# A long-convolution layer and an MLP on one Trainium2 core: wider PSUM pieces in front, an inverse transform with the data as weights, and the second layer norm moved into the MLP

## The chip, the cores and the metric

The kernel runs on one core of one Trainium2 chip. A core has five engines, each of which takes its own instructions strictly in program order: TensorE (PE in the profile, its weight loads PEld), VectorE (DVE), ScalarE (ACT), GpSimd (POOL) and SyncE (SP, which here only issues transfers). They meet through semaphores. Matrix products land in PSUM[...]; TensorE writes to it, VectorE and ScalarE read it[...]. All other tiles lie in SBUF. The metric is the time on the device in microseconds.

## The reference

Sequence S = 2048, width D = 512, MLP width 1376, all inputs bf16.

```python
x = A_q
k_shift = sum over t < 4 of k_pad[:, t:t+S, :] * shift_k[:, 3 - t]
kv = k_shift * v
y = irfft(rfft(kv, 2S) * rfft(ssm_k, 2S))[:S] + kv * ssm_D
h = x + layernorm(x) * y
out = h + relu(layernorm(h) @ w1) @ w2
```

So there is a causal long convolution of every channel with its own filter of 2048 taps, a gate by a layer norm of x, and an MLP behind a second layer norm. The layer norms have no weights of their own.

## The kernel before, in words

The convolution is a Fourier transform of length 4096 in two steps, written as matrix products. Each channel's 2048 times are seen as 32 rows of 64, and the transform goes over the rows (`stage1`), then over the 64 columns with the twiddle factors in the matrices `cc`, `cs` and `cn` (`stage2`). Two channels share the 128 partitions.

1. **Front.** `to_rows` (L195) turns the filter around with 64 transposes on TensorE. `stage1` (L207) transforms it, with four row groups of TensorE side by side: 64 matmuls per group `gb`, into four PSUM tiles of one bank, each copied to SBUF by ScalarE ("A") or VectorE ("D") as a string says. Between the groups, `taps` (L255) makes the four-tap convolution of k on TensorE, and VectorE multiplies it by v. `to_rows` and `stage1` then treat the product kv in the same way (with twice the columns, `wide`). `stage2` of the filter stands in between (L283 to L289): its results go to `kf` in pairs.
2. **Product** (L308 to L340). For each of 16 pairs of frequencies TensorE makes `u`, ScalarE copies a part of it for GpSimd (L317), VectorE and GpSimd multiply it by `kf` (L321), TensorE adds the parts up (L331), and ScalarE writes the result back to `kf` (L333).
3. **Inverse 1** (L389 to L400). 128 matmuls with `kf` as the weights and the two matrices `dre` and `dim` as the moving side; 32 copies to `bp`. Beside it the tables for the last step (`ecore`) are made: whole numbers by GpSimd and VectorE (`ec_turns`), sines by ScalarE (`ec_sins`). The loads of x, w1 and w2 are issued ahead of it on SP's queue.
4. **Inverse 2** (`inv2`, L412). For each of four quarters `q` of the tokens, 256 fp32 matmuls of 32x32 with the table as the weights; ScalarE copies the result, tokens in the partitions, to `zt`.
5. **Gate and MLP.** `ln1` makes the layer norm of x (statistics and normalising on VectorE, `rstd` on GpSimd), `gate` the residual, `hln_` the second layer norm, `transposes` (L466) turn it around on TensorE. `mlp1` and `mlp2` then run quarter by quarter, 44 matmuls of 512 columns each, and every output is added to its residual by VectorE (L501) and stored by SP. The transposes of the next quarter stand in the middle of `mlp2` as a `hook`.

The schedule is manual: on each engine the instructions run in the order in which the program writes them. So an instruction that waits holds everything that its engine has behind it. Dependencies between engines follow from the tiles that the instructions read and write, and a pool's number of buffers says how far a producer may run ahead. The framework puts in the waits.

Of the kernel before, what the change touches and what calls it, by code (L numbers as in the profile page):

```python
# [56 lines left out]
def kernel(  # L57
# [33 lines left out]
    psum = pl.push("psF", bufs=8, space=PSUM)  # L91
# [6 lines left out]
    dtab = consts.tile([P, DC, 64], BF16, name="dtab")  # L98
    for dp in range(2):
        src = bass.AP(tensor=A_ssm_D.tensor, offset=A_ssm_D.offset + 64 * dp, ap=[[0, 64], [P, DC], [1, 64]])  # L100
        nc.scalar.dma_start(out=dtab[64 * dp:64 * dp + 64, :, :], in_=src)
# [93 lines left out]
    def to_rows(src, q, fl, eng):  # L195
        pst = psum.tile([P, 8, P], BF16, tag="ps", name="pst")
        for i in range(8):
            nc.tensor.transpose(out=pst[:, i, :], in_=src[:, :, :, 8 * q + i], identity=ident[:])  # L198
        copy(eng, fl[:, :, :, 8 * q:8 * q + 8], pst[:].rearrange("p i (d g) -> p g d i", d=2))
# [7 lines left out]
    def stage1(fl, a_out, engs, between=None, wide=False):  # L207

        for gb in range(8):
            pss = [psum.tile([P, 8, 64], F32, tag="ps", name=f"ps1_{r}") for r in range(4)]  # L210
            for gi in range(8):
                for f, first in ((f1hi, True), (f1lo, False)):
                    for rg in range(4):
                        rows = slice(32 * rg, 32 * rg + 32)
                        w = 2 if wide and gi < 7 else 1
                        nc.tensor.matmul(out=pss[rg][:, gi:gi + w, :].rearrange("p g c -> p (g c)"),  # L216
                                         lhsT=fl[rows, 8 * gb + gi, :, :].rearrange("p d n -> p (d n)"),
                                         rhs=f[rows, 0:64 * w], start=first, stop=not first,
                                         tile_position=(32 * rg, 0), skip_group_check=wide)
            for rg in range(4):  # L220
                j0 = 64 * rg + 8 * gb
                copy(engs[(4 * gb + rg) % len(engs)], a_out[:, :, j0:j0 + 8], pss[rg][:].rearrange("p g c -> p c g"))
            if between is not None:
                between(gb)
# [23 lines left out]
    dre = consts.tile([P, 2, P], F32R, name="dre")  # L248
    dim = consts.tile([P, 2, P], F32R, name="dim")
# [5 lines left out]
    def taps(u):  # L255
        c, rg = divmod(u, DC)
        ps = psum.tile([P, CH], F32, tag="ps", name="pkv")
        for j in range(KS):
            nc.tensor.matmul(out=ps[:], lhsT=wdiag[:, rg, j, :], rhs=kT[c][:, rg, 16 - j:CH + 16 - j],  # L259
                             start=(j == 0), stop=(j == KS - 1))  # L260
        vv = vT[:, rg, CH * c:CH * c + CH]
        nc.vector.tensor_tensor(out=vv, in0=ps[:], in1=vv, op=ALU.mult)

    def two_taps(gb):
        taps(2 * gb)
        taps(2 * gb + 1)

    stage1(kfl, a1k, "ADAADADA", two_taps)
    for pq in halves:
        for dst, rho, blk, sgn in ((dre, 0, 0, 1.0), (dre, 1, 1, 1.0), (dim, 0, 1, -1.0), (dim, 1, 0, 1.0)):  # L270
            nc.gpsimd.tensor_single_scalar(out=dst[pq, rho, pq], in_=dsc[pq, blk, :], scalar=sgn / 2048, op=ALU.mult)
# [10 lines left out]
    dcol = dtab[:].rearrange("p r g -> p (r g)").unsqueeze(2).to_broadcast([P, 256, 2])  # L282
    for kp in range(16):  # L283
        ks = slice(2 * kp, 2 * kp + 2)
        ps = [psum.tile([P, 2, 256], F32, tag="ps", name=f"ps2k{s}") for s in range(2)]
        for s in range(2):
            stage2(ps[s], a1k, kp, s)
        nc.vector.tensor_tensor(out=kf[:, 0, :, ks], in0=ps[0][:].rearrange("p k j -> p j k"), in1=dcol, op=ALU.add)
        nc.scalar.copy(out=kf[:, 1, :, ks], in_=ps[1][:].rearrange("p k j -> p j k"))  # L289

    a1x = slotA.tile([P, 64, 256], F32R, tag="A", name="a1x")
    stage1(xfl, a1x, "ADADADAA", wide=True)
# [54 lines left out]
    xh = late.tile([P, NT, D], BF16, name="xh")  # L347
    for a, src in enumerate(_tokens(x_d, 0, NT)):
        nc.sync.dma_start(out=xh[32 * a:32 * a + 32, :, :].rearrange("p t d -> p (t d)"), in_=src)
    w1 = late.tile([P, DC, DFF], BF16, name="w1")  # L350
    w2 = late.tile([P, NFC, D], BF16, name="w2")
    nc.sync.dma_start(out=w1[:], in_=B_w1.rearrange("(c p) f -> p c f", p=P))
    nfull = DFF // P
    nc.sync.dma_start(out=w2[:, 0:nfull, :], in_=B_w2[0:nfull * P, :].rearrange("(c p) d -> p c d", p=P))
    if DFF % P:
        nc.sync.dma_start(out=w2[0:DFF % P, nfull, :], in_=B_w2[nfull * P:DFF, :])
    ecore = late.tile([P, 2, 64, 32], F32, name="ecore")
# [4 lines left out]
    rstd2 = late.tile([P, NT, 1], F32, name="rstd2")  # L362
    mhalf = late.tile([P, 4], F32, name="mhalf")
    nc.gpsimd.memset(mhalf[:], -0.5)
    tmpc = pl.push("tmpc", side="right")
    psum = pl.push("psI", bufs=8, space=PSUM)
    k1i = tmpc.tile([P, 1], I32, name="k1i")
    for s in range(0, P, 32):
        nc.gpsimd.iota(k1i[s:s + 32, :], pattern=[[0, 1]], base=1, channel_multiplier=2)
    k1o = tmpc.tile([P, 1], F32, name="k1o")  # L370
    nc.vector.tensor_copy(out=k1o[:], in_=k1i[:])
    ect = {}

    def ec_turns(h):
        r4 = tmpc.tile([P, 16, 32], I32, tag="ec_r", name="ec_r", bufs=4)
        nc.gpsimd.iota(r4[:], pattern=[[1, 16], [64, 32]], base=16 * h, channel_multiplier=0)
        for quarter in (True, False):
            t = tmpc.tile([P, 16, 32], I32, tag=f"ec_t{quarter}", name="ec_t", bufs=2)
            _turns(nc, t[:], r4[:], k1o[:], 8192, quarter)
            ect[h, quarter] = t  # L380

    def ec_sins(h):
        hs = slice(16 * h, 16 * h + 16)
        _sin(ecore[:, 0, hs, :], ect[h, True][:], 8192)
        _sin(ecore[:, 1, hs, :], ect[h, False][:], 8192, neg=True)

    ec_turns(0)
    bp = slotA.tile([P, 64, 2, 2, 64], F32, tag="A", name="bp")
    for b in range(32):  # L389
        ps = psum.tile([P, 2, 2 * P], F32, tag="ps", name="psi1")  # L390
        for i in range(2):
            m = 2 * b + i
            for c, d in ((0, dre), (1, dim)):
                nc.tensor.matmul(out=ps[:, i, :], lhsT=kf[:, c, 4 * m:4 * m + 4, :].rearrange("p r k -> p (r k)"),  # L394
                                 rhs=d[:].rearrange("p a b -> p (a b)"), start=(c == 0), stop=(c == 1))
        copy("ADAADADA"[b % 8], bp[:, 2 * b:2 * b + 2, :, :, :].rearrange("p g a b c -> p g (a b c)"), ps[:])
        if b in (3, 10, 17):
            ec_turns((b + 4) // 7)
        if b in (4, 12, 20, 28):
            ec_sins((b - 4) // 8)  # L400
    pl.pop("tmpc")
    pl.pop("slotB")
    pl.pop("psI")


    psum = pl.push("psZ", bufs=2, space=PSUM)
    ep = pl.push("ep", bufs=2)
    hp = pl.push("hp")
    hlnT = hp.tile([P, DC, NT * P], BF16, name="hlnT")
    zt = hp.tile([P, NT, D], BF16, name="zt")  # L410

    def inv2(q):  # L412
        pz = psum.tile([P, 4, 4, P], F32, tag="pz", name="pz")
        for l4 in range(4):
            for rho in range(2):
                for a in range(4):
                    n2 = 16 * a + 4 * q + l4
                    for r4 in range(4):
                        rows = slice(32 * r4, 32 * r4 + 32)
                        rhs = bp[rows, :, rho, :, n2].rearrange("p (r g) d -> p r d g", r=DC)  # L420
                        nc.tensor.matmul(out=pz[32 * a:32 * a + 32, r4, l4, :], lhsT=ecore[rows, rho, n2, :], rhs=rhs,  # L421
                                         start=(rho == 0), stop=(rho == 1), tile_position=(32 * r4, 32 * a),
                                         skip_group_check=True)
        for l4 in range(4):
            nc.scalar.copy(out=zt[:, 4 * q + l4, :].rearrange("p (m r) -> p m r", r=4),  # L425
                           in_=pz[:, :, l4, :].rearrange("p r m -> p m r"))
# [5 lines left out]

    def stats(mv, q):
        for i in range(4):
            nc.vector.bn_stats(out=st[:, i, :], in_=xh[:, 4 * q + i, :])  # L435
        for i in range(4):
            nc.vector.bn_aggr(out=mv[:, 4 * q + i, :], in_=st[:, i, :])  # L437

    def norm(dst, mv, r, q):
        for i in range(4):  # L440
            t = 4 * q + i
            nc.vector.tensor_scalar(out=dst[:, i, :], in0=xh[:, t, :], scalar1=mv[:, t, 0:1], scalar2=r[:, t, :],
                                    op0=ALU.subtract, op1=ALU.mult)

# [113 lines left out]
```

## Time and profile before

| | |
|---|---|
| three runs, us | 245.87, 244.7, 245.92; median 245.87 |
| the profiled execution: its span, us | 244.7 (the lowest of the three times) |
| TensorE busy | 209.5 us, 86% of the span, 3088 matmuls |
| VectorE, ScalarE, GpSimd busy | 153.1, 132.7, 65.3 us |
| share of the last chain, TensorE | 80% |
| mean granted TensorE clock | 0.968 |

In the lines of the profile, L is a line of the kernel. A group is written as output<-inputs with the number of instructions, the busy time and the mean of one in ns, and then the time for which its engine stood idle just before such instructions, with what ended it. "issue" is a wait for which the profile shows no cause. In the 40 slices each digit is a tenth of busy time, for PEclk a tenth of the full clock; one slice is 6.1 us.

### The profile page before, as it was taken

The page shows a single profiled execution, that of the slowest core. Times are in us where ns is not written, and L with a number is a line of the kernel's source. Part 1 is how long each engine was busy: PE and PEld are TensorE (multiplying, and loading weights), DVE is VectorE, ACT ScalarE, POOL GpSimd, SP SyncE. Part 2 cuts the span into 40 slices and gives each one's busy share as a digit, 9 for nine tenths or more (in the row PEclk, how much of TensorE's full clock was granted, in tenths as well). Part 3 has the DMA queues.
Part 4 walks back from the last instruction along what each step waited for, and adds up shares of the span by engine and source line. Part 5 has one row for each costly group of instructions (what it writes and reads, how often), then busy time and mean ns, then how long its engine had stood idle before and what let it go on. Part 6 is the DMA issues. An engine that isn't in the chain of part 4 may idle for free.

```text
span 244.7 us, 7171 instructions
## 1 busy us (share of the span) xinstructions
PE 209.5 (86%) x3088; PEld 144.7 (59%) x3104; DVE 153.1 (63%) x296; ACT 132.7 (54%) x232; POOL 65.3 (27%) x94
## 2 busy tenths in 40 slices
PE   0586998999857999989988786499999999999992
PEld 0573546999646999969975464334544544454440
DVE  7986987967636989959975778200247747751031
ACT  3878554666765888879943321636226136335500
POOL 6499600000004999971010221000002202200000
PEclk9999999999997999999999999559999999999998
DMA  6999910000000000039970000000110011012011
GB/s 211 302 202 168 144 34 3 4 0 0 5 3 5 1 0 0 3 74 209 279 250 3 5 5 5 0 0 0 30 48 11 0 44 46 0 34 56 0 43 43
DMA packets 23663, 13.88 MB, mean 57 GB/s; under 512 B 19056, under 2 KB 22480, under 8 KB 23504
## 3 DMA queue, kind: packets, MB, share of 16 engines
q1 hardware_dynamic: 22560, 13.36, 24.3%
q8 instruction: 24, 0.39, 0.7%
q10 hardware_dynamic: 1072, 0.07, 0.4%
q14 instruction: 7, 0.06, 0.1%
HBM read 7.08 MB, written 2.10 MB: 38 GB/s over the span
## 4 chain that ended last, share of the span: by engine, by line
PE 80%; ACT 9%; issue 4%; DMA 3%; DVE 2%; ACTq 0%
PE ps1m L485 17%; PE ps2m L498 15%; PE pz L421 9%; PE psi L394 6%; PE pst L198 5%; PE psy L331 5%; PE pkv L259 4%; PE ps L216 4%; PE u L231 4%; DMA sk<-in_A_ssm_k_dram 3%; PE u L233 3%; PE ps2k L233 3%; PE ps2k L231 3%; ACT a1x L203 2%; ACT c2c L174 2%
## 5 line engine op out<-in xcount | busy, mean ns | idle before, releaser
L485 PE MATMUL ps1m<-hlnT,w 128*128 128x512 bf16 (+1 forms) x175 | 41.2, 397 | 1.5 <-ACT hlnT L473 1.3
L487 ACT ACTIVATE h1T<-ps1m 128x512 bf16<-128x512 f32 (+1 forms) x44 | 26.2, 597 | 27.1 <-PE ps1m L485 27.1
L501 DVE TENSOR_TENSOR o<-ps2m,xh 128x512 bf16<-128x512 f32 x16 | 10.9, 690 | 47.9 <-PE ps2m L498 47.9
L498 PE MATMUL ps2m<-w,h1T 128*128 128x512 bf16 (+1 forms) x169 | 38.8, 379 | 0.4
L485 PEld LDWEIGHTS <-w 128*128 128x128 bf16 (+1 forms) x176 | 18.2, 104 | 24.0 <-issue 5.4
L321 DVE TENSOR_TENSOR t<-u,kf 128x704 fp32r<-128x704 f32 x32 | 26.8, 887 | 4.4 <-ACT usb L317 4.4
L321 POOL TENSOR_TENSOR t<-usb,kf 128x320 fp32r<-128x320 f32 x32 | 28.4, 927 | 3.0 <-ACT usb L317 2.4
L498 PEld LDWEIGHTS <-h1T 128*128 128x128 bf16 (+1 forms) x176 | 17.1, 98 | 20.0
L421 PE MATMUL pz<-bp,ecore 32*32 32x128 f32 x1024 | 22.0, 384 | 6.6 <-issue 5.7
L430 POOL TENSOR_SCALAR rstd<-mv 128x4 f32<-128x4 f32 x8 | 1.8, 229 | 92.2 <-DVE mv L437 92.2
L421 PEld LDWEIGHTS pz<-bp,ecore 32*32 32x32 f32 x1024 | 15.2, 103 | 13.2 <-issue 8.9
L425 ACT CAST zt<-pz 128x512 bf16<-128x512 f32 x16 | 8.2, 600 | 21.6 <-PE pz L421 21.6
L435 DVE BATCH_NORM_STATS2 st<-xh 128x6 f32<-128x512 bf16 x32 | 19.7, 683 | 0.0
L333 ACT CAST kf<-psy 128x512 fp32r<-128x512 f32 x32 | 18.4, 646 | 1.6
L394 PE MATMUL psi<-dre,kf 128*128 128x256 f32 x64 | 15.8, 287 | 0.8 <-ACT kf L333 0.8
L473 ACT COPY hlnT<-pt 128x1024 bf16<-128x1024 bf16 x8 | 7.7, 1015 | 15.0 <-PE pt L472 15.0
L331 PE MATMUL psy<-t,ipos 128*128 128x512 f32 x48 | 15.8, 390 | 0.0
L394 PE MATMUL psi<-dim,kf 128*128 128x256 f32 x64 | 15.4, 282 | 0.0
L259 PE MATMUL pkv<-kT,wdiag 128*128 128x512 bf16 x56 | 14.8, 381 | 0.4
L198 PE MATMUL pst<-ident,sk 128*128 128x128 bf16 x64 | 6.7, 295 | 9.1 <-DMA sk<-in_A_ssm_k_dram 9.1
L203 ACT CAST a1k<-ps 128x512 fp32r<-128x512 f32 x20 | 10.4, 593 | 7.1 <-PE ps L216 7.1
L289 ACT CAST kf<-ps2k 128x512 fp32r<-128x512 f32 x16 | 10.3, 641 | 5.4 <-PE ps2k L233 5.3
(107 smaller groups left out, 426.7 us busy)
## 6 DMA issues: line engine op xcount, KB each, us to landing
sk<-in_A_ssm_k_dram SPq DMA_DIRECT2D x1, 2048.0 KB, 8.3
xh<-in_A_q_dram SPq DMA_DIRECT2D x4, 512.0 KB, 8.4
out_dram<-o SPq DMA_DIRECT2D x64, 32.0 KB, 1.6
w<-in_B_w_dram SPq DMA_DIRECT2D x1, 1376.0 KB, 15.1
w<-in_B_w_dram SPq DMA_DIRECT2D x1, 1280.0 KB, 18.3
w<-in_B_w_dram SPq DMA_DIRECT2D x1, 96.0 KB, 17.9
dtab<-in_A_ssm_D_dram ACTq DMA_DIRECT2D x2, 32.0 KB, 8.3
kT<-in_A_k_dram SPq DMA_TRANSPOSE x4, 6.5
```

Of the source, the lines that this page charges most:

```text
L198: nc.tensor.transpose(out=pst[:, i, :], in_=src[:, :, :, 8 * q + i], identity=ident[:])
L231: nc.tensor.matmul(out=ps[:, kk, :], lhsT=w_re[:, k1, :], rhs=a_in[:, k1, :], start=True, stop=False, skip_group_check=True)
L259: nc.tensor.matmul(out=ps[:], lhsT=wdiag[:, rg, j, :], rhs=kT[c][:, rg, 16 - j:CH + 16 - j], start=(j == 0), stop=(j == KS - 1))
L321: eng.tensor_tensor(out=t[:, :, j, :], in0=in0.unsqueeze(1).to_broadcast([P, 2, n, 2]), in1=kfr[:, :, j, ks], op=ALU.mult)
L331: nc.tensor.matmul(out=psy[:], lhsT=m_[:], rhs=t_.rearrange("p j k -> p (j k)"), start=first, stop=not first)
L333: nc.scalar.copy(out=kf[:, s, :, 2 * kp:2 * kp + 2], in_=psy[:].rearrange("p (j k) -> p j k", k=2))
L394: nc.tensor.matmul(out=ps[:, i, :], lhsT=kf[:, c, 4 * m:4 * m + 4, :].rearrange("p r k -> p (r k)"), rhs=d[:].rearrange("p a b -> p (a b)" ...
L421: nc.tensor.matmul(out=pz[32 * a:32 * a + 32, r4, l4, :], lhsT=ecore[rows, rho, n2, :], rhs=rhs, start=(rho == 0), stop=(rho == 1), tile_p ...
L435: nc.vector.bn_stats(out=st[:, i, :], in_=xh[:, 4 * q + i, :])
L485: nc.tensor.matmul(out=ps1[:fsz, :], lhsT=w1[:, c, fc * P:fc * P + fsz], rhs=hlnT[:, c, sc * SCW:(sc + 1) * SCW], start=(c == 0), stop=(c ...
L487: nc.scalar.activation(out=h1T[:fsz, fc, :], in_=ps1[:fsz, :], func=ACT.Relu)
L498: nc.tensor.matmul(out=ps2[:], lhsT=h1T[:ksz, fc, i * P:(i + 1) * P], rhs=w2[:ksz, fc, :], start=(fc == 0), stop=(fc == NFC - 1))
```

## The change

The front works on PSUM tiles of two banks, four of them instead of eight of one; copies, tap products and `kf` pieces have 1024 elements per partition instead of 512. Channels are interleaved four by four, so that four neighbours in a product belong to four row groups. `dre` and `dim` get an order in which the two channel halves stand apart.

Inverse 1 writes `ax`, sixteen pieces of 1024. Inverse 2 takes this data as its weights and the table `ecore` as its moving side, in fp32r, so that its result has the channels in the partitions, as `mlp1` wants them. x and the layer norm of x are brought into that layout by transposing transfers from SBUF to SBUF (`rows_T`, all on SP). `gate` works there, straight out of PSUM; the result goes to `mlp1` without a transpose, and a further transfer brings it back for the residual and its statistics. The second layer norm is folded: w1 loses its column means (`column_means` on TensorE, `center` on VectorE, four pieces), and the factor `rstd2` multiplies the output of `mlp2`. Quarter 0 of inverse 2 runs ahead of the MLP; the others are cut into steps that `hooks` puts between the matmuls of the MLP, two steps a time. GpSimd takes over the multiplication in `ec_turns`. x is loaded in four quarters on SP, w2 is loaded later on ScalarE's queue.

```diff
-    psum = pl.push("psF", bufs=8, space=PSUM)
+    psum = pl.push("psF", bufs=4, space=PSUM)
...
+    nc.gpsimd.tensor_copy(out=dtab[:], in_=draw[:].rearrange("p r g -> p g r"))
...
+    def bank2(name):
+        return psum.tile([P, 2, 512], F32, tag="ps", name=name)
...
+    def stage1(fl, a_out, gb, engs, wide=False):
+
+        pss = [bank2("ps1") for _ in range(2)]
+        outs = [pss[rg // 2][:, rg % 2, :] for rg in range(4)]
...
+        for h in range(2):
+            copy(engs[h], a_out[:, :, 32 * gb:32 * gb + 32].rearrange("p c (g r) -> p r c g", r=DC)[:, 2 * h:2 * h + 2],
+                 pss[h][:].rearrange("p r (g c) -> p r c g", c=64))
...
+    for gb in range(8):
+        stage1(kfl, a1k, gb, "AD" if gb in (2, 4, 6) else "AA")
+        taps(gb // 2, gb % 2)
...
+    for k4 in range(8):
+        ks = slice(4 * k4, 4 * k4 + 4)
         for s in range(2):
...
+            if s == 0:
+                nc.vector.tensor_tensor(out=kf[:, 0, :, ks], in0=pj, in1=dcol, op=ALU.add)
+            else:
+                nc.scalar.copy(out=kf[:, 1, :, ks], in_=pj)
...
+    for gb in range(8):
+        stage1(xfl, a1x, gb, ("AD", "AD", "AA", "AD")[gb % 4], wide=True)
...
+    load_x(0)
     nc.sync.dma_start(out=w1[:], in_=B_w1.rearrange("(c p) f -> p c f", p=P))
...
+    for q in range(1, 4):
+        load_x(q)
...
+    psum = pl.push("psI", bufs=3, space=PSUM)
+    psum1 = pl.push("psC", bufs=2, space=PSUM)
...
+    def ec_turns(q):
+        r4 = late.tile([P, 4, 4, 32], I32, tag="ec_r", name="ec_r", bufs=1)
+        nc.gpsimd.iota(r4[:], pattern=[[1, 4], [16, 4], [64, 32]], base=4 * q, channel_multiplier=0)
...
+        for h, t in ((0, t4[:]), (1, r)):
+            nc.gpsimd.tensor_scalar(out=t, in0=r, scalar1=k1o[:], scalar2=float(4096 + (0 if h else 2048)),
+                                    op0=ALU.mult, op1=ALU.add)
...
+    def ec_wrap(q):
+        for t in ect[q]:
+            nc.vector.tensor_single_scalar(out=t, in_=t, scalar=8191, op=ALU.bitwise_and)
...
+    def rows_T(dst, src):
+        nc.sync.dma_start_transpose(out=dst[:].rearrange("p i r t -> p (i r) t"),
+                                    in_=src.rearrange("p i d -> p (i d)"))
...
+    def lift(q):
+        xT[q] = late.tile([P, 4, DC, P], BF16, tag="xT", name=f"xT{q}", bufs=3)
+        rows_T(xT[q], xh[q][:])
 
     def ln1(q):
...
+        stats(xh[q][:], mv1, rstd1, q)
+        qln = norm1(q)
+        qT[q] = late.tile([P, 4, DC, P], BF16, tag="qT", name=f"qT{q}", bufs=2)
+        rows_T(qT[q], qln[:])
...
+    for b in range(16):
+        inv1(b)
+        if b == 1:
+            lift(0)
+            ec_wrap(0)
+        if b == 3:
+            ln1(0)
+        if b == 6:
+            ec_sins(0)
+            ec_turns(1)
+        if b in (8, 9):
+            column_means(b - 8)
+            center(b - 8)
+        if b in (11, 12):
+            column_means(b - 9)
+        if b == 11:
+            lift(1)
+            ec_wrap(1)
+    ec_sins(1)
...
+    def gate(q, i):
+        pz = pzs[q][:].rearrange("p r (i a) n -> p r i (a n)", i=4)
+        nc.vector.tensor_tensor(out=qT[q][:, i, :, :], in0=pz[:, :, i, :], in1=qT[q][:, i, :, :], op=ALU.mult)
+        nc.vector.tensor_tensor(out=xT[q][:, i, :, :], in0=qT[q][:, i, :, :], in1=xT[q][:, i, :, :], op=ALU.add)
+
+    def inv2(q, j, width):
+        if j == 0:
+            pzs[q] = psz.tile([P, DC, 16, 32], F32, tag="pz", name="pz")
+        pz = pzs[q]
+        n2 = 16 * (j % 4) + 4 * q + j // 4
+        w = min(width, 16 - j)
+        for rho in range(2):
+            for rg in range(DC):
+                rows = slice(32 * rg, 32 * rg + 32)
+                nc.tensor.matmul(out=pz[:, rg, j:j + w, :].rearrange("p a b -> p (a b)"),
+                                 lhsT=ax[rows, 64 * rho + n2, :, :].rearrange("p d g -> p (d g)"),
+                                 rhs=ecore[rows, rho, q, j:j + w, :].rearrange("p a b -> p (a b)"),
+                                 start=(rho == 0), stop=(rho == 1), tile_position=(32 * rg, 0), skip_group_check=True)
+        if j % 4 == 3:
+            gate(q, j // 4)
+        if j == 15:
+            hT[q] = xT[q]
+            nc.sync.dma_start_transpose(out=xh[q][:].rearrange("p i (r c) -> p (i r) c", r=DC),
+                                        in_=hT[q][:].rearrange("p i r t -> p (i r t)"))
+
+    def hooks(q, n):
+        todo = list(range(16))
+
+        def step():
+            for _ in range(n):
+                if todo:
+                    inv2(q, todo.pop(0), 4)
+        return step
+
+    def mlp1(sc, hook=None):
...
+            if hook is not None and fc >= 1:
+                hook()
...
+                if hook is not None and fc % 3 == 2:
+                    hook()
...
+            nc.vector.scalar_tensor_tensor(out=o[:], in0=ps2[:], scalar=rstd2[:, t, :], in1=xh[sc][:, i, :],
+                                           op0=ALU.mult, op1=ALU.add)
...
+    psz = pl.push("psZ", space=PSUM)
+    psm = pl.push("psM", bufs=4, space=PSUM)
+    for j in range(16):
+        inv2(0, j, 8)
+    center(2)
+    center(3)
+    ln1(1)
+    ec_turns(2)
+    ec_wrap(2)
+    lift(2)
+    stats(xh[0][:], mv2, rstd2, 0)
+    mlp1(0, hooks(1, 2))
+    ec_sins(2)
+    ec_turns(3)
+    ec_wrap(3)
+    ln1(2)
+    lift(3)
+    mlp2(0, hooks(2, 2))
+    ec_sins(3)
+    stats(xh[1][:], mv2, rstd2, 1)
+    ln1(3)
+    mlp1(1)
+    mlp2(1, hooks(3, 2))
+    stats(xh[2][:], mv2, rstd2, 2)
+    mlp1(2)
+    mlp2(2)
+    stats(xh[3][:], mv2, rstd2, 3)
+    mlp1(3)
+    mlp2(3)
```

## The prediction

> **What bounds the kernel now.** I read the page's slices first, then the chain that ended last, then stages and waits.
>
> ```profile
> PE   0586998999857999989988786499999999999992
> PEclk9999999999997999999999999559999999999998
> PE 80%; ACT 9%; issue 4%; DMA 3%; DVE 2%; ACTq 0%
> L421 PE MATMUL pz<-bp,ecore 32*32 32x128 f32 x1024 | 22.0, 384 | 6.6 <-issue 5.7
> L435 DVE BATCH_NORM_STATS2 st<-xh 128x6 f32<-128x512 bf16 x32 | 19.7, 683 | 0.0
> ```
>
> TensorE carries 80% of the chain, and its weak slices are the second inverse stage (L421) and the cold start of the MLP after it. Busy time by stage, in the columns PE, PEld, DVE, ACT, POOL, clock, DMA share, GB/s:
>
> ```profile
> 108.30:125.30 17.00, 16.00 (x128) 15.50 (x128) 15.88 (x31) 15.13 (x29) 2.76 (x5) 1.00 0.99 262
> 125.30:153.00 27.70, 22.01 (x1024) 15.18 (x1024) 19.83 (x59) 6.16 (x12) 4.71 (x8) 1.00 0.08 22
> 153.00:158.30 5.30, 1.86 (x17) 1.71 (x17) 1.38 (x4) 3.98 (x6) 0.35 (x1) 0.58 0.00 0
> 158.30:170.80 12.50, 12.26 (x44) 5.15 (x46) 0.00 (x0) 5.97 (x10) 0.00 (x0) 0.77 0.00 0
> 190.70:240.10 49.40, 49.05 (x247) 23.31 (x250) 21.51 (x56) 17.57 (x27) 3.76 (x6) 1.00 0.11 29
> ```
>
> Inverse 1 takes 17 us, inverse 2 28 us, the join to the MLP 5 us, and then the MLP is solid TensorE: 44 matmuls of 0.216 us (9.5 us) per half, 76 us for eight halves. L421's "issue" gaps come every 3.45 us, after some 118 matmuls:
>
> ```profile
> 137.12 2.74 PE pz L421 x112
> 139.86 0.82 issue
> 140.68 2.69 PE pz L421 x119
> ```
>
> The lines that decide my forecast are two of the product stage:
>
> ```profile
> 89.25 0.73 ACT L317 COPY usb<-u 128x160 f32<-128x160 f32 x2
> 89.59 0.89 DVE L321 TENSOR_TENSOR t<-u,kf 128x704 fp32r<-128x704 f32 x1 [0.20 <-ACT usb L317]
> ```
>
> VectorE reads columns of u that ScalarE's copy doesn't touch, and nothing that it writes. u's last matmul began at 88.84 and took 0.28; VectorE still starts only when the copy is over. Two engines on one PSUM bank go one after the other, even on separate columns (DVE waits so 12 times, 4.4 us).
>
> [...] 118 to 128 matmuls with their weight loads per 3.45 us. [...] clock 0.58 from 153 to 158.3, and the next 44 matmuls take 12.5 us instead of 9.5. [...] fp32r at 256 columns is spaced 0.12 us; no row shows 128 columns.
>
> **Front.** Stage 1, taps and row transposes keep their matmuls; evictions double in size (512 elements 0.59 ACT, 0.69 DVE; 1024 about 1.03 and 1.22) and 8 single banks become 4 pairs. Group 0 is now all ACT's ("AA"), and ACT is busy with the table until 21.06: two copies end at 23.0, so the second taps start at 23.1 instead of 22.2 (+0.9). The last taps' product is one piece of 1.22 instead of two of 0.69, the first of which was covered (+0.55). Stage 2 stays at 128 x 0.12. In the second stage 1 the 512 matmuls still bring 1024 instructions[...], so larger evictions gain nothing there; its last copies are A, A, A of 1.03 (+0.5). Front: +1.95; [...] ten ACT copies of 1.03 would bound the second stage 1 at 10.3 instead of its 14.5, so -2 is the other end. The draw copy on POOL hides under taps (POOL idles from 29 us). The product is unchanged; inverse 1 starts at 108.36 + 1.95 = 110.3.
>
> **Inverse 1.** PE is still 16 x 8 x 0.12 = 15.4 us, plus column_means 4 x 0.6. ACT has 12 copies at 1.0 plus four sines of 0.7, DVE 4 copies of 1.23; only three buffers. In DVE's queue now: wrap (0.9), which waits for POOL's turns (iota 0.72, two tensor_scalars of 512 elements; from L192's 2.78 for 1024, 1.55 each, bounds 1.1 to 3.1; I take 1.55: 3.8 in all); then copy 3, then ln1(0): statistics 2.84, rstd 1.5 on POOL, norm 1.38. Copy 7 sits behind that until 123.5, and PE, out of buffers, waits 1.8 us at b=10; both centers (1376 elements from PSUM, 1.55 each) come before copy 11. By these queues, ax is complete at 131.9 (before: 125.3). The x loads, w1 and the first transposes share DMA: 3.4 MB at 262 GB/s is 13 us after 109.5; lift(0) and qT(0) follow, each 2 to 3.5 us of SP and 5.2 to 6.8 to landing as kT and vT show (SBUF sources aren't shown: bounds 5 to 8, I take 3.2 and 5.6). qT(0) lands at 131.3: just covered. If that cover goes, each us late is a us.
>
> **Inverse 2.** Gone: the 28 us with its 16 evictions, 64 transposes and their copies, hln. Quarter 0 alone now stands ahead of the MLP: 32 groups of four row tiles; ps2k's spacing of 0.12 gives 3.8 us. But gate(q,i) reads all four banks of pz (psZ has one buffer) while j = 4, 8, 12 write to them. By the bank order, four steps (0.96), gate's product (0.66, with 0.3 of latency) alternate: 4 x 1.9. The add (0.36) follows; mlp1(0) starts at 139.9, 18.4 us earlier than now.
>
> **The MLP with hooks.** 24 hooks of two steps: four groups of 0.12 (bounds 0.066 if 128 columns set it[...]; I take the spacing of ps2k, whose weights have the same 128 columns), and two changes of tiling mode, 0.11 each from the gaps between ps L216 and pkv L259: 0.70 per hook, 16.8 us. In before's layout nothing of that lay in the MLP but 2.7 us of transposes.
>
> Then the wait that the change adds. inv2(1, 4), in the hook after fc = 3, must wait for gate(1,0), and behind it in PE's order stands all of mlp1(0). DVE's order before gate(1,0), from 139.8: center(2), center(3) 3.1; ln1(1) 2.84 + 1.42 + 1.38, to 148.6; wrap(2), which waits for POOL's turns(2), themselves behind rstd, to 151.9; statistics of quarter 0's result 2.84, to 154.8; gate 155.4 (qT(1) lands at 154.2). PE stands from 144.8 to 155.5: 10.7 us. mlp1(0) ends at 139.9 + 9.5 + 8 x 0.7 + 10.7 = 165.7. mlp2(0): sines(2) come behind the last relu (1.5 us of wait), POOL's turns(3) behind these, 171.6; wrap 172.6; ln1(2) to 178.2; qT(2) lands 183.9; gate(2,0) 184.7. PE stands from 170.4 to 184.8: 14.4 us. mlp2(0) ends at 165.7 + 15.1 + 15.9 = 196.6. mlp1(1) 206.1. ln1(3) comes behind the last output and the next statistics: qT(3) lands 211.5, PE waits 3.1; mlp2(1) ends 224.3. Four clear halves: 262.3. The tail of before (240.1 to 244.7) 4.6: 266.9. The output's product with rstd stays one DVE pass of 0.69, hidden under 2.4 us of matmuls. w2's load moves to ACT's queue at 131, 1.5 us of issue, 8 to landing: hidden until mlp2(0). The back transposes and lifts on SP stand before output stores, which wait anyway.
>
> [...] 3.0 us were lost after the one of before; I take half of that each, +3. Sum: 244.7 + 1.95 (front) + 6.6 - 1.95 (inverse 1) + (139.9 - 131.9) - 33.0 (125.3 to 158.3) + 127.0 (139.9 to 266.9, own tail) - 86.4 + 3 = 269.9. It stands against the profiled execution, whose span of 244.7 is also its time, the lowest of the three; the median is 1.2 above. **Predicted: 270 us.**
>
> **Rivals.**
> - *Gates do not hold PE* (the order is by address, and adjacent columns don't wait). Then mlp1(0) runs 137.3 to 152.4, pz's single buffer costs some 3 us, mlp2(0) ends at 170.3; outputs stand behind gate(2,0) in DVE's queue and hold mlp1(1)'s buffers, so that it ends at 184.9; the kernel ends at 242.9, 240.1 with cheap groups, 246 with a cooled clock: not slower. The sign turns where the 29.7 us of PE waits fall below about 7. For it: a gate reads only finished columns. Against: DVE t behind ACT usb. 0.14.
> - *The small fp32r matmuls or POOL's turns are dearer.* At 0.27 a group each hook costs 0.6 more, and later gates: 277.8 + 3 = 281. With turns of 6.9 us: 276 + 3. For: neither is in the profile. Against: [...] L192 the slope. 0.10.
> - *The front gains*: the second stage 1 falls to 10.3, so that the front gives -2 instead of +1.95: 266. Against it: L216 stops for "issue", not for copies. Inside the range of my own case.
>
> **How the numbers follow.** My case, 0.76: 259 (cheap groups, turns of 3.0, landing in 5) to 278 (landing in 8, SP 6 each), most of it 262 to 276. Adding the rivals' 0.14 at 240 to 246 and 0.10 at 277 to 282, and leaving out a tenth at each end, the range is 243 to 281; the likeliest case's own is 260 to 278. A measurement here can tell about 0.5% (1.2 us around 245.9) from no change. Faster is two thirds of the first rival, 0.09; same the rest of it, 0.04; slower 0.87.
>
> **What would show it.** In the changed trace: PE idle of some 10 us within ps1m of quarter 0 and 14 us in ps2m, released by DVE's gate; DVE's gate waiting on the transpose of qT; clock near 0.5 after each; pz in groups of four 0.12 apart; second stage 1 still 12.6 us of PE with gaps. Wrong if pz's j = 4 starts before gate's product ends, if gates come early because qT lands by 145, or if pz costs under 5 us in all.

## The result, and the profile after

The changed kernel takes 283.55 us (median of four, 281.06 to 286.14) against 245.86 us: ratio 1.149, 95% interval [1.141, 1.157]. Forecast were 270, slower, with a range of 243 to 281: the sign held, the size did not. All ratios below are to runs of the kernel before on the same chip; executions in which the chip was disturbed count in the medians but not in the ratios, and the traces of e5_hoist_contig and e8_last_copy are of such executions. The profiled execution took 284.15 us with a span of 282.4.

The slices and the chain of the changed kernel, as shown of before (one slice is now 7.1 us):

```profile
PE   0666888998466999998773949830999989999993
PEclk9997999999975999999965675995579999999999
PE 44%; DVE 11%; DMA 5%; ACT 3%; POOL 3%; issue 2%; ACTq 0%; DVEq 0%
```

TensorE has fallen from 80% to 44% of the chain (a third of the chain is not attributed to an engine). The "30" in the 27th and 28th slices is a standstill within the MLP, and the slow clock now appears for longer between stage 1 and the product (12th and 13th slices), around inverse 2 and twice within the MLP. TensorE's two largest waits behind inverse 1, from the list of waits (us in total, times, longest):

```profile
PE pz L513 <- DVE qT L501: 19.0, 6, 11.0
PE ps1m L540 <- DVE w L441: 4.2, 1, 4.2
```

By stretch (same columns as before): quarter 0 of inverse 2 with the wait behind it, mlp1(0) up to its standstill, the standstill, what follows, the second standstill, what follows that.

```profile
141.20:155.00 13.80, 7.16 (x128) 6.45 (x129) 7.47 (x11) 0.00 (x0) 0.00 (x0) 0.55 0.65 165
155.00:162.30 7.30, 7.21 (x48) 3.08 (x47) 5.80 (x15) 1.79 (x3) 3.56 (x5) 0.67 0.12 23
162.30:166.50 4.20, 0.00 (x0) 0.00 (x0) 3.24 (x9) 0.60 (x1) 1.27 (x2) 1.00 1.11 206
166.50:181.50 15.00, 14.95 (x125) 7.74 (x126) 3.77 (x7) 3.58 (x6) 0.00 (x0) 0.66 0.07 13
186.00:197.00 11.00, 0.03 (x1) 0.00 (x0) 5.00 (x14) 0.74 (x2) 1.27 (x2) 0.70 0.41 76
197.00:214.00 17.00, 16.94 (x134) 8.52 (x135) 6.31 (x12) 0.00 (x0) 0.00 (x0) 0.69 0.23 48
```

And the two hooks on either side of the first standstill:

```profile
160.63 0.67 PE L513 MATMUL pz<-ecore,ax 32*128 32x128 f32 x16
166.55 1.12 PE L513 MATMUL pz<-ecore,ax 32*128 32x128 f32 x16 [4.29 <-DVE qT L501]
```

So the standstills that I forecast are there, at the forecast places. What I had not forecast is in front of them: stage 1's evictions. First two groups of the kernel before, then four of the changed kernel.

```profile
L203 ACT CAST a1k<-ps 128x512 fp32r<-128x512 f32 x20 | 10.4, 593 | 7.1 <-PE ps L216 7.1
L205 DVE CAST a1x<-ps 128x512 fp32r<-128x512 f32 x12 | 7.5, 685 | 6.0 <-PE ps L216 6.0
```

```profile
L201 ACT CAST a1k<-ps 128x1024 fp32r<-128x1024 f32 x13 | 23.8, 1964 | 2.4 <-PE ps L223 2.4
L201 ACT CAST a1x<-ps 128x1024 fp32r<-128x1024 f32 x10 | 18.2, 2016 | 0.1
L203 DVE CAST a1x<-ps 128x1024 fp32r<-128x1024 f32 x6 | 11.6, 1962 | 5.2 <-PE ps L223 4.4 <-ACT kf L296 0.8
L201 ACT CAST ax<-psi 128x1024 fp32r<-128x1024 f32 x12 | 11.8, 1013 | 6.6 <-PE psi L462 6.6
```

The last line is inverse 1's eviction: the same engine, helper, size and types in 1.01 us. Stage 1's takes twice that on ScalarE, and on VectorE 1.96 us for inverse 1's 1.22. In the second stage 1 ScalarE is busy for 18.2 us with 0.1 us of idleness: it is the bound there. The other evictions of this size run as I assumed them (1.01 us on ScalarE, 1.22 on VectorE). What sets stage 1's apart is the place in SBUF: with channel j = 4g + r, a half writes single 4-byte elements 16 bytes apart, where before runs of eight lay side by side.

### The profile page after: what moved, and what is told of

It reads as the page before. It is cut to its first block, busy times and chain, and to the rows that moved or that the text cites. A ratio compares the mean times of both kernels' runs of the same rounds, so it can differ in the third digit from the quotient of the medians.

```text
span 282.4 us, 5994 instructions
## 1 busy us (share of the span) xinstructions
PE 222.9 (79%) x2544; PEld 150.6 (53%) x2544; DVE 156.2 (55%) x236; ACT 137.6 (49%) x175; POOL 72.5 (26%) x105
## 4 chain that ended last, share of the span: by engine, by line
PE 44%; DVE 11%; DMA 5%; ACT 3%; POOL 3%; issue 2%; ACTq 0%; DVEq 0%
PE ps2m L553 14%; PE ps1m L540 10%; PE pz L513 8%; DMA qT<-qln 5%; PE psy L339 4%; DVE st L410 4%; PE u L236 3%; PE u L238 3%; DVE qln L423 2%; DVE qT L501 2%; DVE w L441 2%; POOL rstd L406 1%; ACT ax L201 1%; ACT kf L341 1%; PE psi L462 1%
## 5 line engine op out<-in xcount | busy, mean ns | idle before, releaser
L540 PE MATMUL ps1m<-xT,w 128*128 128x512 bf16 (+1 forms) x176 | 44.6, 409 | 4.2 <-DVE w L441 4.2
L553 PE MATMUL ps2m<-w,h1T 128*128 128x512 bf16 (+1 forms) x176 | 44.4, 399 | 0.0
L513 PE MATMUL pz<-ecore,ax 32*128 32x128 f32 (+7 forms) x512 | 27.3, 347 | 21.4 <-DVE qT L501 19.0
L513 PEld LDWEIGHTS pz<-ecore,ax 32*128 32x128 f32 x512 | 22.8, 248 | 35.8 <-DVE qT L501 22.6
L501 DVE TENSOR_TENSOR qT<-pz,qT 128x512 bf16<-128x512 f32 x16 | 11.1, 692 | 37.3 <-PE pz L513 27.4
L558 DVE SCALAR_TENSOR_TENSOR o<-ps2m,rstd,xh 128x512 bf16<-128x512 f32 x16 | 12.0, 750 | 32.6 <-PE ps2m L553 32.5
L201 ACT CAST a1k<-ps 128x1024 fp32r<-128x1024 f32 x13 | 23.8, 1964 | 2.4 <-PE ps L223 2.4
L201 ACT CAST a1x<-ps 128x1024 fp32r<-128x1024 f32 x10 | 18.2, 2016 | 0.1
L267 DVE TENSOR_TENSOR vT<-pkv,vT 128x1024 bf16<-128x1024 f32 x8 | 9.8, 1224 | 12.6 <-PE pkv L264 12.6
L201 ACT CAST ax<-psi 128x1024 fp32r<-128x1024 f32 x12 | 11.8, 1013 | 6.6 <-PE psi L462 6.6
```

What stands on the lines that cost most here:

```text
L201: nc.scalar.copy(out=o, in_=i)
L501: nc.vector.tensor_tensor(out=qT[q][:, i, :, :], in0=pz[:, :, i, :], in1=qT[q][:, i, :, :], op=ALU.mult)
L513: nc.tensor.matmul(out=pz[:, rg, j:j + w, :].rearrange("p a b -> p (a b)"), lhsT=ax[rows, 64 * rho + n2, :, :].rearrange("p d g -> p (d g) ...
L540: nc.tensor.matmul(out=ps1[:fsz, :].rearrange("p (i t) -> p i t", i=4), lhsT=w1[:, c, fc * P:fc * P + fsz], rhs=hT[sc][:, :, c, :], start= ...
L553: nc.tensor.matmul(out=ps2[:], lhsT=h1T[:ksz, fc, i * P:(i + 1) * P], rhs=w2[:ksz, fc, :], start=(fc == 0), stop=(fc == NFC - 1))
```

## The experiments

Two theories, one for each part of the loss. **Stride**: single elements 16 bytes apart double stage 1's evictions, which costs the front 9 to 10 us. **Gate's order**: TensorE waits for gates that wait for q, and pays again in a slow clock. Their rivals: the width and pairing of PSUM tiles or the fetching of instructions; and that the layer norms and transposes hold the MLP up whatever TensorE waits for.

### The stride alone, in the kernel before

```diff
-                j0 = 64 * rg + 8 * gb
-                copy(..., a_out[:, :, j0:j0 + 8], ...)
+                copy(..., a_out[:].rearrange("p c (g r) -> p r c g", r=4)[:, rg, :, 8 * gb:8 * gb + 8], ...)
...                                              # and the product's evictions put the order back
```

> The kernel before, in which only the order of channels between the front and the product is changed: the four 512-element copies of each stage 1 block keep their size, their engines and their eight PSUM banks, but write single 4-byte elements 16 bytes apart (channel 4g+r) instead of runs of eight. The order is put back where the product's evictions are written. Stride theory: the copies rise from 0.60 us (ScalarE) and 0.69 us (VectorE) to about 1.0 us; the second stage 1, where ScalarE has 20 of the 32 copies, becomes bound by them and grows from 14.5 to some 20 us, and the whole kernel by 5 to 9 us, to about 251 to 255. Rival (width and pairing: the wide copies of the changed kernel are slow because 1024 elements over two banks are read and only four such pairs fit): the copies stay at 0.6 and 0.7 us, and the time within 1 us of before.

Measured: 253.99 us, ratio 1.031 [1.024, 1.039]. The groups of this kernel:

```profile
L203 ACT CAST a1k<-ps 128x512 fp32r<-128x512 f32 x20 | 18.9, 1116 | 1.8 <-PE ps L216 1.7
L203 ACT CAST a1x<-ps 128x512 fp32r<-128x512 f32 x20 | 18.1, 1159 | 0.4 <-PE ps L216 0.4
L205 DVE CAST a1x<-ps 128x512 fp32r<-128x512 f32 x12 | 11.9, 1070 | 4.7 <-PE ps L216 4.7
```

In the kernel before they were 593, 607 and 685 ns. Size, banks, the order of reading and the number of TensorE's instructions are unchanged, and the product's evictions, which put the order back, take 646 ns as before. So neither the width nor the fetching of instructions is needed: the writing pattern does it, and it is worth 8 us even there.

### The changed kernel without the stride

```diff
-            copy(engs[h], a_out[:, :, 32 * gb:32 * gb + 32].rearrange("p c (g r) -> p r c g", r=DC)[:, 2 * h:2 * h + 2],
+            copy(engs[h], a_out[:].rearrange("p c (r g) -> p r c g", r=DC)[:, 2 * h:2 * h + 2, :, 8 * gb:8 * gb + 8],
...
-            nc.scalar.copy(out=kf[:, s, :, 2 * kp:2 * kp + 2], in_=psy[:].rearrange("p (j k) -> p j k", k=2))
+            nc.scalar.copy(out=kf[:, s, :, 2 * kp:2 * kp + 2].rearrange("p (g r) k -> p g r k", r=DC),
+                           in_=psy[:].rearrange("p (r g k) -> p g r k", r=DC, k=2))
```

> The changed kernel, in which only the order of channels is changed: stage 1 still evicts 128x1024 from two banks with four such tiles, but writes runs of eight elements (channel 64r+g), and the product's evictions read PSUM in the order that inverse 1 wants. Stride theory: the stage 1 copies fall from 1.96 to 2.02 us to about 1.03 (ScalarE) and 1.22 us (VectorE), inverse 1 starts at about 110 instead of 120 us, and the kernel takes 272 to 276 us. Rival (width, pairing or fetching of instructions): the copies stay near 2 us or the blocks take as long without them, and the kernel stays at 282 to 285 us.

Measured: 274.97 us, ratio 1.116 [1.106, 1.125]. The evictions take 1.01 to 1.02 us on ScalarE and 1.22 us on VectorE, and inverse 1 starts at 110.7 instead of 120.4 us. ScalarE's first group:

```profile
L201 ACT CAST a1k<-ps 128x1024 fp32r<-128x1024 f32 x13 | 12.6, 1013 | 6.0 <-PE ps L223 6.0
```

### Pairs instead of single elements

```diff
-  a_out[...].rearrange("p c (g r) -> p r c g", r=DC)[:, 2 * h:2 * h + 2],  pss[h][:].rearrange("p r (g c) -> p r c g", c=64)
+  a_out[...].rearrange("p c (g r) -> p c g r", r=DC)[:, :, :, 2 * h:2 * h + 2],  pss[h][:].rearrange("p r (g c) -> p c g r", c=64)
```

> The changed kernel with the order of elements within stage 1's evictions alone changed: the two channels of a half, which lie side by side in SBUF, are written one after the other, so that runs of 8 bytes are written 16 bytes apart where single elements of 4 bytes were. The addresses, sizes and engines stay. If a price is paid for each run (each jump of the address), the copies fall to about half of what the jumps cost: from 1.96 and 2.02 us to between 1.0 and 1.5 us, and the kernel by 4 to 9 us to 275 to 280. If it is the 16 bytes that each group of four elements spans which cost, whatever part of them is written, the copies stay at 1.9 to 2.0 us and the kernel at 282 to 285.

Measured: 271.01 us, ratio 1.101 [1.095, 1.106], below what either theory had forecast.

```profile
L201 ACT CAST a1x<-ps 128x1024 fp32r<-128x1024 f32 x10 | 10.1, 1074 | 2.9 <-PE ps L223 2.9
L203 DVE CAST a1x<-ps 128x1024 fp32r<-128x1024 f32 x6 | 7.2, 1223 | 5.7 <-PE ps L223 4.9 <-ACT kf L296 0.8
```

The same addresses are written; only two neighbours now follow each other (and PSUM is read in the order that fits). That takes away nearly the whole doubling: 2.02 to 1.07 us on ScalarE, 1.96 to 1.22 on VectorE. The second theory, that the copies stay at 1.9 to 2.0 us, falls. A price for each jump would have left half of the doubling, some 1.5 us on ScalarE; the band of 1.0 to 1.5 us that I had given it was wider than that, and the measured copies lie in it. With single elements 16 bytes apart the wide evictions take 1.9 to 2.0 ns an element; on ScalarE it is 1.03 to 1.05 with two neighbours in succession and 0.99 in runs of eight. Why two are enough isn't shown.

### ScalarE between TensorE and the gate

```diff
-        nc.vector.tensor_tensor(out=qT[q][:, i, :, :], in0=pz[:, :, i, :], in1=qT[q][:, i, :, :], op=ALU.mult)
+        zs = mp.tile([P, DC, P], BF16, tag="zs", name="zs", bufs=4)
+        nc.scalar.copy(out=zs[:], in_=pz[:, :, i, :])
+        nc.vector.tensor_tensor(out=qT[q][:, i, :, :], in0=zs[:], in1=qT[q][:, i, :, :], op=ALU.mult)
```

> The changed kernel with one step put between inverse 2 and the gate: ScalarE, idle for most of the MLP, copies each group of four columns from PSUM to a bf16 tile, and VectorE's gate reads that. TensorE then waits for ScalarE's copy (some 0.6 us) and no longer for the transposed q nor for VectorE's queue. Theory of the gate's order: the waits of PE for the gate (19 us of idle time) nearly all go, and with them the slow clock after them: 258 to 266 us. Rival (the layer-norm and transposes are what the MLP waits for in any case): the same standstill comes back as a wait for the gated tokens, and the time falls by at most 5 us, to 278 to 284.

Measured: 261.32 us, ratio 1.058 [1.049, 1.068]. In its waits, TensorE's for VectorE's gate (19.0 us in the changed kernel) are gone, and what it waits for ScalarE's copies is 2.1 us in all:

```profile
PE pz L515 <- ACT zs L502: 2.1, 3, 0.7
PE ps1m L542 <- DVE w L441: 4.6, 1, 4.6
```

The rival falls: TensorE stood still because the gate read from the banks into which TensorE had to go on. With the tile emptied by an engine that was idle, the late q delays the gate, but not the MLP. The wait for the centering of w1 stays.

### The same gate, its inputs earlier

```diff
+        if b in (13, 14):
+            center(b - 11)
...
+            stats(xh[1][:], mv1, rstd1, 1)   # beside inverse 1
...
+    ln1b(1)                                  # the rest of ln1(1), ahead of quarter 0
...
-    mlp1(0, hooks(1, 2))
+    mlp1(0, hooks(1, 2), early_2)            # ec_sins(2), ec_turns(3), ln1(2), lift(3) within mlp1(0)
-    mlp2(0, hooks(2, 2))
+    mlp2(0, hooks(2, 2), early_3)            # ec_sins(3), ln1(3) within mlp2(0)
```

> The changed kernel with the same instructions in another order: layer norm 1 of quarters 1, 2 and 3, their transposes, the turns and the sines go out one stage earlier, the last two centerings of w1 before inverse 2 rather than behind its first gates, and the statistics for layer norm 2 behind the gates. The gate stays on the PSUM tile itself. Theory of the gate's order: what PE waits for is only that q comes late, so the standstills of 4.2 us before the MLP and of 4.3, 11 and 2.2 us within it shrink to below 1 us each and the clock stays up: 258 to 266 us. Rival (queues are full in any case, so work put earlier delays other work): a wait of the same size turns up elsewhere, 278 to 284.

Measured: 262.09 us, ratio 1.065 [1.058, 1.072].

```profile
PE pz L520 <- DVE ax L203: 5.0, 1, 5.0
PE pz L520 <- DVE qT L508: 4.5, 5, 1.9
PE ps1m L547 <- DVE xT L509: 1.3, 1, 1.3
```

The waits for the gate fall from 19.0 to 4.5 us, with the gate still on the PSUM tile. But the rival had a point: a wait of 5.0 us for inverse 1's last copy is new, because VectorE now has statistics and centering in front of it. Two different remedies of one cause gain 22 and 21 us; in the 21 is also that the wait of 4.2 us for the centering has gone from in front of mlp1(0), less the new one.

### Together

e4_both is e1_contig with e2_actz, and `center` at b = 13 and 14. e5_hoist_contig is e1_contig with e3_hoist. e6_all is all three, and:

```diff
-        copy("D" if b % 4 == 3 else "A", ax[:, :, :, 4 * b:4 * b + 4],
+        copy("D" if b in (3, 15) else "A", ax[:, :, :, 4 * b:4 * b + 4],
```

> The changed kernel with both causes undone and one wait more: stage 1 writes runs of eight elements as in e1_contig, ScalarE copies inverse 2's groups for the gate as in e2_actz, and the last two centerings of w1 are put into inverse 1, so that mlp1(0) doesn't wait 4.6 us for them. If the two causes are separate, their gains add: 261.3 - 8.6 - 4 = 248 to 250 us. If the front's gain is eaten in the MLP (x, w1 and w2 arrive no earlier), 254 or more.

> The changed kernel with stage 1 written in runs of eight as in e1_contig and the earlier layer norms of e3_hoist; the gate stays on the PSUM tile. Separate causes: 262.1 - 8.6 = 252 to 255 us. If the earlier work is pushed together by the earlier front, 256 or more.

> e1_contig, e2_actz and e3_hoist together, and ScalarE takes two more of inverse 1's copies (the 8th and the 12th), so that VectorE's layer norm 1 and centering stand before no copy. Separate causes: what e4_both gives less 1 to 3 us for the standstill left in front of mlp1(1) and for the copies, 245 to 249 us. If VectorE's queue bounds the stretch from inverse 1 to mlp1(0), the earlier layer norm 1 of quarter 1 holds quarter 0's gates up and it isn't faster than e4_both.

Measured: 249.06 us, ratio 1.014 [1.007, 1.021]; 252.97 us, 1.025 [1.014, 1.036]; 245.55 us, 0.997 [0.995, 1.000]. All three are where the sums put them, so the gains add: the two causes are separate. With both undone and the centering moved (e4_both), 34.5 of the 37.7 us of loss are gone; that the kernel then draws level with the one before takes e6_all, with earlier layer norms and two copies on another engine besides. In e6_all TensorE still waits 2.1 us for inverse 1's last copy, and its quarter 0 takes 1.2 to 2.1 us for each 32 matmuls at a clock of 0.57.

```diff
-        inv2(0, j, 8)                                  # and inv2(q, todo.pop(0), 4) in the hooks
+        inv2(0, j, 1)                                  # and inv2(q, todo.pop(0), 1)
...
-        if j == 0:
+        if j == 0 or (q == 0 and j % 4 == 0):          # two pz tiles in turn for quarter 0
```

> e6_all with inverse 2's matmuls one column group wide instead of four or eight (32 moving columns instead of 128 or 256, the rest were overwritten later), and with two PSUM tiles in turn for quarter 0, so that TensorE goes on while ScalarE copies. If the moving columns set the time of quarter 0 (2.0 us for each 32 matmuls at a clock of 0.59), its groups fall to about 1 us and the waits of 0.7 us go: 3 to 5 us faster than e6_all, 241 to 245 us. If the weight loads set it (187 to 248 ns each, four row groups side by side), only the waits go, some 2 us, and the hooks in the MLP stay at 0.55 to 0.60 us.

Measured: 240.49 us, ratio 0.978 [0.970, 0.985]: faster than the kernel before, by 1.5 to 3.0%. From its timeline, inverse 2's quarter 0 and two hooks:

```profile
132.86 6.04 PE L523 MATMUL pz<-ecore,ax 32*128 32x32 f32 x128 [3.87 <-DVE ax L203]
145.61 0.62 PE L523 MATMUL pz<-ecore,ax 32*128 32x32 f32 x16
147.14 0.62 PE L523 MATMUL pz<-ecore,ax 32*128 32x32 f32 x16
```

Quarter 0 takes 6.0 us of TensorE in one piece instead of four pieces of 1.2 to 2.1 us with 0.7 us between them. The hooks hardly change (0.62 us; 0.67 with 128 columns at full clock), so there it is not the moving columns that set the time. What the narrow matmuls and what the two tiles gave quarter 0 isn't separated: both were changed at once, and the clock over its 6.0 us was 0.59. In e6_all the first 32 matmuls of 256 columns, still at full clock, took 1.22 us.

```diff
-        copy("D" if b in (3, 15) else "A", ax[:, :, :, 4 * b:4 * b + 4],
+        copy("D" if b in (3, 7) else "A", ax[:, :, :, 4 * b:4 * b + 4],      # and ec_sins(1) behind quarter 0
```

> e7_narrow with one order changed: inverse 1's last copy goes to ScalarE (VectorE has the 4th and the 8th instead), and the sines of quarter 1 come after quarter 0's copies. In e7_narrow TensorE waited 3.9 us for that copy, which stood behind the centering of w1 on VectorE. If that wait set the start of inverse 2, it starts some 2.5 us earlier and the kernel takes 237.5 to 239 us; if VectorE's queue (centering, then layer norm 1 of quarter 1, then the gates) sets the start of mlp1(0) in any case, 240 to 241.

Measured: 241.68 us, ratio 0.981 [0.975, 0.987], no gain over e7_narrow. The wait has only changed its name:

```profile
PE pz L522 <- DVE w L445: 2.7, 1, 2.7
```

TensorE now waits for the centering itself: its column means lie in PSUM banks that quarter 0's tiles take over. In both orders TensorE waits for work in VectorE's queue; the length of the wait is read from an execution of 252.64 us and isn't compared.

e11_pairs_all is e7_narrow with the pairs of e9_pairs in place of the order of e1_contig.

> e7_narrow with stage 1 written in pairs as in e9_pairs, in place of the other order of channels of e1_contig, so that the product's evictions are again those of the changed kernel. e9_pairs was 4 us faster than e1_contig; that came from a higher clock in the product and in quarter 0 of inverse 2 (0.80 there against 0.61), not from the copies. If this is the permuted reading of the product's evictions, the gain carries over and the kernel takes 236 to 239 us; if it is chance in when the clock falls, it takes what e7_narrow took, 239.5 to 241.

Measured: ratio 0.985 [0.979, 0.990]. The 4 us by which e9_pairs was ahead of e1_contig didn't carry over, and they were not clear of noise: the two ratios were taken on different chips, and their intervals touch at 1.106. The intervals of e7_narrow, e8_last_copy and e11_pairs_all overlap, and I can't rank them.

### The slow clock by itself

```diff
+                    if q < 3 and todo[0] == 4:
+                        warm = psm.tile([P, 512], F32, tag="ps", name="warm")
+                        for k in range(16 if q == 1 else 42):
+                            nc.tensor.matmul(out=warm[...], lhsT=w1[:, 0, 0:P], rhs=hT[0][:, :, 0, :], start=True, stop=True)
                     inv2(q, todo.pop(0), 4)
```

> The changed kernel with matmuls that serve nothing put in front of the two places where TensorE stands still for the gate: 16 of 512 columns (some 3.8 us at full clock) in mlp1(0), 42 (some 10 us) in mlp2(0). No wait is removed. If the standstills cost twice, once as idle time and once in the slow clock after them (0.66 over the 15 us after the first, 0.69 over the 17 us after the second), TensorE now comes out of them at full clock and the kernel is 6 to 10 us faster, 274 to 278 us, though it has more work. If the slow stretches have another cause, it stays at 282 to 285, or rises where the extra matmuls outlast the standstill.

Measured: 280.89 us, ratio 1.143 [1.135, 1.150], which overlaps the changed kernel's interval: the forecast of 274 to 278 us was missed, and no gain is shown. Stretches of this kernel after the first and after the second standstill, then the first two hooks after the second:

```profile
168.00:181.50 13.50, 12.58 (x148) 6.76 (x148) 4.05 (x8) 6.12 (x10) 2.24 (x3) 1.00 0.29 40
190.50:192.30 1.80, 0.01 (x4) 0.01 (x4) 0.72 (x2) 0.00 (x0) 0.00 (x0) 1.00 0.60 115
193.20:200.00 6.80, 6.80 (x59) 3.55 (x57) 1.87 (x3) 0.00 (x0) 0.00 (x0) 0.55 0.25 52
```

```profile
192.29 0.67 PE L513 MATMUL pz<-ecore,ax 32*128 32x128 f32 x16 [1.82 <-DVE qT L501]
194.21 1.12 PE L513 MATMUL pz<-ecore,ax 32*128 32x128 f32 x16
```

After the first, where 1.3 us of pause were left, the clock stays at 1.00 instead of 0.66: shown for this place. After the second, where the matmuls ended 1.8 us too early, TensorE restarted at full clock, and 1.6 us later the clock fell all the same. So half of the test succeeded.

The traces say more about when the clock changes. In all fourteen of them it is either 1.00 or 0.50 (the values between are means over both), and the time from one change to the next is, 102 times out of 102, a whole multiple of 3.41 us to within 0.01 us. In the changed kernel it changes at 142.7, 159.8, 166.6, 176.8, 190.5 and 207.5 us: 5, 2, 3, 4 and 5 steps apart. So the clock can fall after TensorE has restarted (here 1.6 us after), and where the steps fall against the program differs from run to run. There the traces of e9_pairs and e1_contig differ. In e1_contig the clock was at half for the first 6 us of the product and fell again at 134.1, within quarter 0, whose later groups took 1.7 to 2.0 us; in e9_pairs the product ran at 1.00, and the clock fell at 137.1, behind quarter 0, whose groups took 1.07 to 1.22 us. Whether a pause brings the fall, and from what length, stays open: the same 1.2 us in mlp2(1) were followed by half clock in e1_contig and e9_pairs, and not in the changed kernel and e10_warm.

## Why the prediction was wrong in size

The direction and the mechanism in the MLP were right; the size was not. In the stages of my sum (us; after: profiled execution):

| step | predicted | after | what it was |
|---|---|---|---|
| start of inverse 1 | 110.3 | 120.4 | evictions of stage 1 |
| inverse 1 to ax complete | 21.6 | 20.6 | nearly as thought |
| quarter 0 to mlp1(0) | 8.0 | 14.1 | clock 0.55; centering |
| mlp1(0) and mlp2(0) | 56.7 | 58.5 | shorter standstills, slow clock |
| mlp1(1) and mlp2(1) | 27.7 | 26.0 | shorter standstill |
| the rest | 42.6 | 42.8 | as thought |
| allowance for the clock | 3.0 | (within the above) | |
| sum | 269.9 | 282.4 | |

The time is another 1.8 us above the span. It is so in every execution that lists both, those of the kernel before among them (1.7 to 1.9 us); so its span of 244.7 and its lowest time of 244.7, which I had taken for one execution, are hardly the same one, and my sum, a span, was held against a time.

**The step that failed: the front.** The prediction put "1024 about 1.03 and 1.22" for all wide evictions, and so +1.95 us for the front, where the runs show +12.0 (120.4 against 108.4): 10.1 of the 12.5 us by which the sum is short. That price was right for `ax`, `kf` and `xfl`; stage 1's measured 1.96 to 2.02 us. The diff shows the new order of channels, and I read it as a matter of layout, without asking how many neighbours one eviction writes at a time. My "rival in the front" went the other way: I allowed a gain of 4 us, and no loss. With the writing mended and nothing else, the changed kernel takes 271.0 us (e9_pairs) or 275.0 us (e1_contig), both inside the 260 to 278 that I gave the likeliest case, and inverse 1 starts at 109.0 or 110.7 us where I had 110.3. That they come so near to 270 is in part luck: behind the front my standstills were some 12 us too long in all and my prices for the clock and the centering too small, and these errors nearly cancel (2.4 us of the 12.5 are left).

**"L216 stops for 'issue', not for copies"** held only with copies at 1.01 to 1.22 us: in e1_contig the matmuls of the second stage 1 end at 74.6 us, before at 73.9, though the copies are wider. With copies at 2.0 us the stage ended with ScalarE's last one at 87.1.

**The gate's order was right.** TensorE stood still at steps j = 4 for 4.3 us in mlp1(0), 11.0 in mlp2(0) and 1.2 in mlp2(1), against 10.7, 14.4 and 3.1 predicted. Removing the gate from that order, or feeding it earlier, gains 21 to 22 us. The first was shorter because TensorE came to it 17.5 us later than I had it (mlp1(0) started 15.2 late, and its first half ran at half clock), and the gate's product ended only 11.1 later (166.5 instead of 155.4): 3 us of centering, which I had counted within the standstill, now stood ahead of mlp1(0), and GpSimd's turns took 0.69 to 0.93 us each, not 1.55. In mlp2(0) the same turns and a landing of q 4.3 to 4.6 us after its issue, not 5.6 (and below my bounds of 5 to 8), made most of the difference.

**The clock was under-sized.** I took 3 us, half of the 3.0 lost after the one hole of before for each of two holes, without a reason for the half. After the two standstills the clock was 0.66 for 15 us and 0.69 for 17: by my estimate 15 x 0.34 + 17 x 0.31 = 10.4 us of full-rate work lost. And quarter 0 itself, small pieces between waits, took 1.22 us for its first group, at full clock, and 1.9 to 2.1 for the other three, at half, where I had put 0.96 by ps2k's spacing. Little idleness went with the half clock there: 1.4 us lay ahead of quarter 0 and 0.8 between its groups. It was little in the kernel before as well: there the clock fell at 153.8, and TensorE had stood still for 1.0 us up to 151.7 and since 153.0. No run here shows a length of idleness from which the clock falls.

**A wait not foreseen.** mlp1(0) waited 4.2 us for the centering of w1, which I had in VectorE's queue behind the last gate, but not in TensorE's way. Moved into inverse 1, that wait is gone (e3_hoist to e7_narrow); 1.3 to 1.6 us for the last gate remain in its place.

**The rivals.** "Gates do not hold PE" fell by the waits. "Small fp32r matmuls or POOL's turns dearer" fell too: a hook takes 0.62 to 0.67 us at full clock, where I had 0.70, and the turns were cheaper than assumed. For fp32r ps2k shows a spacing of 0.12 us for 256 columns, against 0.216 for 512 in bf16: 0.47 and 0.42 ns a column. "The front gains" fell with the evictions.

## What to carry to other kernels

Price an eviction by how it writes as well as by its size: here two fp32 neighbours in succession were enough (2.02 to 1.07 us for 1024 elements on ScalarE), and the order of the loop was changed without moving a single address. Where TensorE returns to a bank that another engine reads, put the engine with an empty queue between them; a late input then delays that consumer only (TensorE's waits went from 19.0 to 2.1 us). And price a standstill of TensorE with the slow clock behind it, which here cost an estimated 10.4 us beside the 15.3 us of the first two standstills themselves.

## What I had not expected of the hardware

- Single 4-byte elements written 16 bytes apart: 1.96 to 2.02 us for 1024 elements and 1.06 to 1.16 us for 512, nearly the same on ScalarE and VectorE, against 1.01 and 1.22, 0.60 and 0.69 us in runs of eight; in runs of two 1.05 to 1.07 and 1.22 us.
- The clock changed on a grid of 3.41 us (102 of 102 times between changes). After both standstills three steps, 10.2 us, in which TensorE was busy throughout went by at half clock, and pauses of 1.8 us (e10_warm) and, in two traces out of four, 1.2 us were followed by half clock.
- Inverse 2's fp32r matmuls with 32 moving columns cost a hook nearly what they cost with 128: 0.62 against 0.67 us for sixteen.
